# The order of the last four output tiles in a fused attention and feed-forward kernel

## Chip, cores and metric

One NeuronCore of a Trainium2 chip runs the whole kernel. The metric is the device time of one execution in microseconds; the time before is the median of three runs.

## What is computed

The input x has 2048 rows of 448 columns. It is normalised per row, and the output is x plus two branches that both read the normalised rows: attention with 16 heads of 28 columns in a causal window of 256 rows, and a gated feed-forward layer of 1792 hidden columns.

```
xn = layernorm(x)
q, k, v = split(xn @ wqkv)                      # 16 heads of 28
A = softmax(q k^T * 28**-0.5, causal, window 256) v @ wo
B = (gelu(xn @ w_gate) * (xn @ w_up)) @ w_down
out = x + A + B
```

All inputs and the output are bfloat16.

## The kernel before

The rows are worked on in four blocks of 512 (`qb` 0 to 3), each of four row tiles of 128, so row tiles 0 to 15. For each block the kernel makes the attention of that block, which ends in `oN` (four groups of 128 partitions by 512 rows, on SBUF), and the hidden layer `hT` (14 groups of 128 by 512). The output of a row tile is then 18 matmuls that add into one PSUM tile `po`: 14 with `hT` and the weights `wd`, four with `oN` and the weights `wo`, each 448 columns wide. `gen_down` issues them, as a generator that yields after every step, so that for blocks 0 to 2 these matmuls are woven into the attention of the block that follows. The order of everything is written out by hand; there is no scheduler.

For the last block (`qb` 3) nothing follows. Its `gen_down` runs alone at the end, after a check value (`flag`) has been made on VectorE. The terms come in three groups: `main` (ten groups of `hT` that are made early), `late` (the four of `hT` that come from the last two gates, made at line 501) and `os` (the four of `oN`, whose last rows arrive by small transfers that SyncE issues at lines 351 and 356, through a buffer in device memory). `part` issues some terms of one tile (line 393), `whole` all of them, and `end` is called behind the last one: VectorE adds the rows of x to `po` into `res` (line 382), `give` hands the PSUM bank back, and SyncE issues the transfer of `res` to the output (line 384). There are two `res` buffers; the second half of the last tile has a buffer of its own (tag `wa`).

Before, the last block begins three tiles (12, 13, 14) in three of the four single PSUM banks: main of 12 and 13, late of 12 and 13, main and late of 14, then the attention terms of the three, each followed by its add and its transfer. Tiles 13 and 14 are issued as two matmuls of 224 columns for each term (`ws`). Tile 15 follows in two halves of 224 columns, each with its 18 terms, its own PSUM bank, its add and its transfer.

After 48 steps of this generator each engine loads the check value into a register (line 887). Behind the generator GpSimd copies from the last result, VectorE writes one value (lines 890 to 892), and every engine branches on the check value at line 897: where it is 1, as here, a long general path is jumped over. Each engine then waits for its queues and meets the others in a closing barrier (line 1018).

A second PSUM pool (`phase[0].pool`, tag `s`) holds two buffers of two banks each; the last tiles that use them are the gates `gt` of the feed-forward layer, read by ScalarE at line 496.

Of the kernel before, what the change touches and what calls it, by code (L numbers as in the profile page):

```python
# [12 lines left out]
bf16 = mybir.dt.bfloat16  # L13
f32 = mybir.dt.float32
i32 = mybir.dt.int32

S, D, H, Dh, F = 2048, 448, 16, 28, 1792
P = 128
NT = S // P
NF = F // P  # L20
QB, NB = 512, 4
# [6 lines left out]
def kernel(  # L28
# [11 lines left out]
    nc = tc.nc  # L40
# [4 lines left out]
    work = fast.enter_context(tc.tile_pool(name="work", bufs=3))  # L45
# [3 lines left out]
    phase = [None]  # L49
# [152 lines left out]
    held = {}  # L202

    def take(name, cols=QB, tag=None):

        tag = tag or spare[0]
        spare.remove(tag)  # L210
        ps = psum.tile([P, QB], f32, name=name, tag=tag, bufs=1)[:, 0:cols]
        held[id(ps)] = tag, ps
        return ps

    def give(*tiles):
        for ps in tiles:
            spare.append(held.pop(id(ps))[0])
# [94 lines left out]
    def gen_pairs(qb, order):  # L312

        def v_pair(t):
            two = [take("pv", D) for _ in range(2)]
            for c in range(7):
                for hi, ps in enumerate(two):
                    r = slice(64 * hi, 64 * hi + 64)
                    w = wv[r, 3, :] if c == 6 else wv[r, c // 2, :] if c % 2 == hi else wvs[r, c // 2, :]
                    nc.tensor.matmul(ps, lhsT=xchunk(qb, hi, c, (t + hi) * P, P), rhs=w, start=c == 0, stop=c == 6,  # L320
                                     tile_position=(64 * hi, 0), skip_group_check=True)
                if c < 6:
                    yield
            for i in range(2):
                v_copy(t + i, two[i], nc.vector.tensor_copy if i or not t % 4 or qb == 1 else nc.scalar.copy)
            yield

        def qk_pair(g):
            two = [take("p" + part) for part in "qk"]
            for c in range(7):  # L330
                for hi, ps in enumerate(two):
                    r, hs = slice(64 * hi, 64 * hi + 64), slice(4 * g, 4 * g + 4)
                    w = w3p[r, hs, :] if c == 6 else (wqp, wkp)[hi][r, c // 2, hs, :] if c % 2 == hi else wsq[r, c // 2, hs, :]
                    nc.tensor.matmul(ps, lhsT=w.rearrange("p h d -> p (h d)"), rhs=xchunk(qb, hi, c, qb * QB, QB), start=c == 0,  # L334
                                     stop=c == 6, tile_position=(64 * hi, 0), skip_group_check=True)
                if c < 6:
                    yield
            qk_copies(qb, g, *two, nc.vector.tensor_copy if (g != 1) == (qb == 1) else nc.scalar.copy)
            yield

        return chain(*(v_pair(4 * qb + n) if kind == "v" else qk_pair(n) for kind, n in order))
# [25 lines left out]
    def gen_down(qb):  # L367

        hT, oN = hTs[qb], oNs[qb]
        fs = [(hT, wd, f) for f in range(NF)]  # L370
        main, late, os = fs[0:5] + fs[7:12], [fs[f] for f in (5, 12, 6, 13)], [(oN, wo, g) for g in range(4)]

        def begin(tt, lo=0, up=D):
            return tt, take("po", up - lo), lo, up

        def end(tt, po, lo, up):
            t, w = 4 * qb + tt, up - lo
            if lo:
                res = work.tile([P, 2 * QB], bf16, name="res", tag="wa", bufs=1)
            else:  # L380
                res = work.tile([P, D], bf16, name="res", bufs=2)
            nc.vector.tensor_tensor(out=res[:, 0:w], in0=po[:, 0:w], in1=x_sb[:, t, lo:up], op=ALU.add)  # L382
            give(po)
            nc.sync.dma_start(out=outv[:, t, lo:up], in_=res[:, 0:w])
            last_res[:] = [res]

        def part(o, terms, start=False, stop=False):
            tt, po, lo, up = o
            w = up - lo
            ws = (0, w // 2, w) if 4 * qb + tt in (NT - 3, NT - 2) else (0, w)  # L390
            for n, (x, wt, k) in enumerate(terms):
                for a, b in zip(ws, ws[1:]):
                    nc.tensor.matmul(po[:, a:b], lhsT=x[:, k, tt * P:(tt + 1) * P], rhs=wt[:, k, lo + a:lo + b],  # L393
                                     start=start and n == a == 0, stop=stop and n == len(terms) - 1, skip_group_check=True)
                if stop and n == len(terms) - 1:
                    end(*o)
                yield

        def whole(terms, *o):
            yield from part(begin(*o), terms, True, True)  # L400

        if qb < NB - 1:
            two = [begin(tt) for tt in range(2)]
            for o in two:
                yield from part(o, main + late, True)
            for o in two:
                yield from part(o, os[0:3])
            for tt, po, *_ in two:
                r = slice(64 * tt, 64 * tt + 64)
                nc.tensor.matmul(po, lhsT=oN[r, 3, tt * P:(tt + 1) * P], rhs=wo[r, 3, :], start=False, stop=True,  # L410
                                 tile_position=(64 * tt, 0), skip_group_check=True)
            for o in two:
                end(*o)
            yield
            for tt in (2, 3):
                yield from whole(main + late + os, tt)
        else:
            three = [begin(tt) for tt in range(3)]
            for terms, start in ((main, True), (late, False)):
                for o in three[0:2]:  # L420
                    yield from part(o, terms, start)
            yield from part(three[2], main + late, True)
            for o in three:
                yield from part(o, os, False, True)
            for lo, up in ((0, D // 2), (D // 2, D)):
                yield from whole(main + late + os, 3, lo, up)

    def new_hT(qb):
        hT = blk.tile([P, NF, QB], bf16, name="hT", tag="hT")
# [369 lines left out]
    for qb in range(NB):  # L799
# [4 lines left out]
        if qb == 0:  # L804
# [3 lines left out]
            w = gen_pairs(1, (("v", 0), ("v", 2), ("k", 0), ("k", 1), ("k", 2)))  # L808
# [4 lines left out]
                    [lambda: stat(11), (w, 7), lambda: rstd(8, 4), "sums", "inverse", (w, 7)]]  # L813
        else:
            d = gen_down(qb - 1)
            if qb < 3:
                u = gen_pairs(qb + 1, (("v", 0), ("k", 0), ("v", 2), ("k", 1), ("k", 2)))
# [64 lines left out]
    nc.vector.tensor_reduce(out=ok1, in_=okr, axis=AX.X, op=ALU.min)  # L882
    nc.vector.tensor_copy(out=flag[:, :], in_=ok1)
    last = gen_down(NB - 1)
    for _ in range(48):
        next(last)
# [136 lines left out]
```

## Time and profile before

| | |
|---|---|
| median of three runs | 214.37 us (214.35 to 214.7) |
| span of the profiled execution | 213.1 us |
| the median less that span | 1.27 us |
| PE busy | 207.6 us, 97% |
| VectorE, ScalarE, GpSimd busy | 157.5, 131.6, 48.6 us |
| output transfers | 15 of 112 KB, 2 of 56 KB |

The profile gives the span from the first to the last instruction, not a device time for that execution; the device time of the runs is 1.27 us longer than the span. PE is TensorE, PEld its weight loads, DVE VectorE, ACT ScalarE, POOL GpSimd, SP SyncE; a q behind the name is the engine's sequencer, which reads the instructions and waits for semaphores ahead of the engine. A row of a timeline gives the start and the length in us, the engine, the line of the kernel, what is written and read, and the count; in brackets stand the idle time before it and who ended it. Queue q1 is that of the transfers, q8 and q14 are loads of instructions.

### The profile page before, as it was taken

The numbers are of one execution on the slowest core, as the hardware profiler recorded it, in microseconds if no ns is written. First come the engines' busy times: TensorE is split into PE (matmuls) and PEld (weight loads), VectorE is DVE, ScalarE is ACT, GpSimd is POOL, SyncE is SP. The second block draws the span as 40 slices with busy tenths as digits, with TensorE's granted clock in tenths as the row PEclk, the third lists the DMA queues.
The fourth block names the chain that finished last, engine by engine and source line by source line (L and its number), as shares of the span: only waits on it lengthen the run. The fifth ranks groups of instructions, "written<-read, shape, count | busy, mean of one in ns | idle before, by whom it ended". The sixth has DMA issues, their size and how long they took to land.

```text
span 213.1 us, 6428 instructions
## 1 busy us (share of the span) xinstructions
PE 207.6 (97%) x2722; PEld 101.2 (47%) x2722; DVE 157.5 (74%) x355; ACT 131.6 (62%) x123; POOL 48.6 (23%) x86
## 2 busy tenths in 40 slices
PE   7999999999999999999999999999999999999992
PEld 2433444444454545444445445444445444544992
DVE  7899998999767985796536997495483898479531
ACT  4699578566777977423777887532676877665000
POOL 5287658451000220041000201022000022006001
PEclk9999999999999999999999999999999999999998
DMA  6999969979420101003421000001000101000011
GB/s 184 280 221 215 106 172 220 243 241 171 110 53 25 37 20 26 8 5 65 74 74 46 25 0 29 20 0 30 16 3 0 47 4 45 6 0 0 26 45 49
DMA packets 23993, 15.67 MB, mean 74 GB/s; under 512 B 9208, under 2 KB 23832, under 8 KB 23960
## 3 DMA queue, kind: packets, MB, share of 16 engines
q1 hardware_dynamic: 22918, 14.87, 31.2%
q8 instruction: 22, 0.36, 0.7%
q10 hardware_dynamic: 1042, 0.34, 0.7%
q14 instruction: 11, 0.09, 0.1%
HBM read 9.26 MB, written 2.41 MB: 55 GB/s over the span
## 4 chain that ended last, share of the span: by engine, by line
PE 94%; DVE 1%; ACT 1%; DMA 1%; issue 1%; DVEq 0%; ACTq 0%
PE po L393 26%; PE gt L456 20%; PE u L456 12%; PE ue L456 8%; PE pq L334 7%; PE sc L652 6%; PE ov L624 5%; PE pv L320 4%; PE pq L191 2%; PE pv L191 1%; DMA x_sb<-in_A_x_dram 1%; ACT p_sb L656 1%; DVE st L155 1%; PE s L191 1%; PE pk L191 1%
## 5 line engine op out<-in xcount | busy, mean ns | idle before, releaser
L656 ACT ACTIVATE p_sb<-sc 128x2048 bf16<-128x2048 f32 x39 | 73.2, 1878 | 20.5 <-PE sc L652 13.5
L496 ACT ACTIVATE p_sb<-gt 128x1024 bf16<-128x1024 f32 x28 | 28.7, 1025 | 33.6 <-PE gt L456 30.7
L591 POOL TENSOR_TENSOR oN<-oc,l 128x512 bf16<-128x512 f32 x16 | 21.5, 1355 | 120.0 <-DVE l L604 120.0
L393 PE MATMUL po<-wd,hT 128*128 128x448 bf16 (+1 forms) x266 | 46.2, 324 | 0.0
L456 PE MATMUL gt<-xnT,wg 64*128 64x512 bf16 x224 | 45.6, 376 | 0.0
L456 PE MATMUL gt<-xsw,wg 64*128 64x512 bf16 x168 | 40.7, 376 | 0.0
L504 DVE TENSOR_TENSOR hT<-p_sb,u 128x512 bf16<-128x512 bf16 x34 | 21.9, 677 | 16.0 <-PE u L456 15.8
L572 DVE TENSOR_TENSOR p_sb<-p_sb,masks 128x256 bf16<-128x256 bf16 (+1 forms) x90 | 27.8, 363 | 7.6 <-ACT p_sb L656 7.6
L393 PEld LDWEIGHTS <-hT 128*128 128x128 bf16 x266 | 24.5, 98 | 16.8 <-issue 2.2
L456 PEld LDWEIGHTS <-wg 64*128 64x128 bf16 x392 | 19.0, 94 | 22.5 <-issue 0.2
L456 PEld LDWEIGHTS <-wu 64*128 64x128 bf16 x392 | 18.7, 94 | 22.4 <-issue 0.8
L456 PE MATMUL u<-xnT,wu 64*128 64x512 bf16 x136 | 28.1, 376 | 0.0
L456 PE MATMUL u<-xsw,wu 64*128 64x512 bf16 x102 | 24.7, 376 | 0.0
L382 DVE TENSOR_TENSOR res<-po,x_sb 128x448 bf16<-128x448 f32 (+1 forms) x17 | 9.8, 592 | 11.6 <-PE po L393 9.3
L456 PE MATMUL ue<-xnT,wu 64*128 64x512 bf16 x88 | 18.0, 377 | 0.0
L652 PE MATMUL sc<-qT,kT 28*64 28x320 bf16 (+7 forms) x648 | 16.4, 261 | 0.1
L456 PE MATMUL ue<-xsw,wu 64*128 64x512 bf16 x66 | 16.4, 377 | 0.0
L582 POOL TENSOR_SCALAR_AFFINE_SELECT p_sb<-p_sb 128x512 bf16<-128x512 bf16 (+1 forms) x21 | 14.2, 702 | 6.6 <-ACT p_sb L656 6.5
L609 DVE TENSOR_TENSOR oc<-oc,ov 128x512 f32<-128x512 f32 x12 | 8.2, 681 | 8.7 <-ACT oc L608 8.7
L652 PEld LDWEIGHTS <-kT 28*64 28x64 bf16 (+1 forms) x648 | 7.5, 102 | 13.3 <-issue 12.0
L393 PE MATMUL po<-wo,oN 128*128 128x448 bf16 (+1 forms) x70 | 13.0, 320 | 0.0
L473 DVE CAST hT<-ue 128x512 bf16<-128x512 f32 x18 | 11.6, 679 | 1.9 <-PE ue L456 1.8
(108 smaller groups left out, 276.9 us busy)
## 6 DMA issues: line engine op xcount, KB each, us to landing
out_dram<-res SPq DMA_DIRECT2D x15, 112.0 KB
x_sb<-in_A_x_dram SPq DMA_DIRECT2D x3, 448.0 KB
wd<-in_B_w_down_dram SPq DMA_DIRECT2D x3, 448.0 KB
xsw<-xnT SPq DMA_DIRECT2D x6, 192.0 KB
wu<-in_B_w_up_dram SPq DMA_DIRECT2D x2, 560.0 KB
wg<-in_B_w_gate_dram SPq DMA_DIRECT2D x2, 448.0 KB
wg<-in_B_w_gate_dram SPq DMA_DIRECT2D x2, 336.0 KB
wraw<-in_A_wqkv_dram SPq DMA_DIRECT2D x2, 252.0 KB
```

What stands on the lines that cost most here:

```text
L334: nc.tensor.matmul(ps, lhsT=w.rearrange("p h d -> p (h d)"), rhs=xchunk(qb, hi, c, qb * QB, QB), start=c == 0, stop=c == 6, tile_position= ...
L393: nc.tensor.matmul(po[:, a:b], lhsT=x[:, k, tt * P:(tt + 1) * P], rhs=wt[:, k, lo + a:lo + b], start=start and n == a == 0, stop=stop and ...
L456: nc.tensor.matmul(ps, lhsT=w[64 * hi:64 * hi + 64, c, p * P:(p + 1) * P], rhs=xchunk(qb, hi, c, qb * QB, QB), start=c == 0, stop=c == 6, ...
L473: copy(out=hTs[qb][:, p + 7 * i, :], in_=us[i])
L496: nc.scalar.activation(out=ges[p][:, :, :], in_=gt[:, :, :], func=ACT.Gelu_apprx_tanh)
L504: nc.vector.tensor_tensor(out=hT[:, p + 7 * i, :], in0=ge[:, i, :], in1=u, op=ALU.mult)
L572: nc.vector.tensor_tensor(out=reg, in0=reg, in1=m, op=ALU.mult)
L582: nc.gpsimd.affine_select(out=reg, in_=reg, pattern=mid + [[1 if diag else -1, min(w, P)]], compare_op=ALU.is_ge, fill=0.0, base=0 if diag ...
L591: nc.gpsimd.tensor_tensor(out=oN[:, g, :], in0=oc[:, :], in1=inv, op=ALU.mult)
L624: nc.tensor.matmul(ov[half or 0][32 * j:32 * j + 32, q0:q0 + nq], lhsT=v_sb[r, kt, 4 * g + j, :], rhs=p_sb[r, j, col:col + nq], start=n == ...
L652: nc.tensor.matmul(ss[k0:k0 + nk, j, col:col + nq], lhsT=kT[r, g, kt * P + k0:kt * P + k0 + nk], rhs=qT[r, g, ring(qb).start + q0:ring(qb) ...
L656: nc.scalar.activation(out=p_sb[:, :, 0:ncol], in_=ss[:, :, 0:ncol], func=ACT.Exp, scale=SCALE)
```

## The change

Only the last block and `end` are touched. Whole tiles are one matmul per term again (`ws` goes, 36 matmuls fewer). Two tiles are begun, not three: main and late of 12 and 13. Tile 15 gets two PSUM tiles in the two-bank pool, `first` and `last`, one for each half. Main and late of `first` come next, then the attention terms of 12, 13 and `first`, each with its add and transfer; then main of `last`; then the whole of tile 14; then the last eight matmuls, late and attention of `last`. There are four `res` buffers. `give` is called only for PSUM tiles that came from `take`.

```diff
             if lo:
                 res = work.tile([P, 2 * QB], bf16, name="res", tag="wa", bufs=1)
             else:
-                res = work.tile([P, D], bf16, name="res", bufs=2)
+                res = work.tile([P, D], bf16, name="res", bufs=4)
             nc.vector.tensor_tensor(out=res[:, 0:w], in0=po[:, 0:w], in1=x_sb[:, t, lo:up], op=ALU.add)
-            give(po)
+            if id(po) in held:
+                give(po)
...
         def part(o, terms, start=False, stop=False):
             tt, po, lo, up = o
             w = up - lo
-            ws = (0, w // 2, w) if 4 * qb + tt in (NT - 3, NT - 2) else (0, w)
             for n, (x, wt, k) in enumerate(terms):
-                for a, b in zip(ws, ws[1:]):
-                    nc.tensor.matmul(po[:, a:b], lhsT=x[:, k, tt * P:(tt + 1) * P], rhs=wt[:, k, lo + a:lo + b],
-                                     start=start and n == a == 0, stop=stop and n == len(terms) - 1, skip_group_check=True)
+                nc.tensor.matmul(po[:, 0:w], lhsT=x[:, k, tt * P:(tt + 1) * P], rhs=wt[:, k, lo:up],
+                                 start=start and n == 0, stop=stop and n == len(terms) - 1, skip_group_check=True)
...
-            three = [begin(tt) for tt in range(3)]
+            two = [begin(tt) for tt in range(2)]
             for terms, start in ((main, True), (late, False)):
-                for o in three[0:2]:
+                for o in two:
                     yield from part(o, terms, start)
-            yield from part(three[2], main + late, True)
-            for o in three:
+            first, last = ((3, phase[0].pool.tile([P, 2, QB], f32, name="pl", tag="s")[:, 0, 0:D // 2], lo, lo + D // 2)
+                           for lo in (0, D // 2))
+            yield from part(first, main + late, True)
+            for o in (*two, first):
                 yield from part(o, os, False, True)
-            for lo, up in ((0, D // 2), (D // 2, D)):
-                yield from whole(main + late + os, 3, lo, up)
+            yield from part(last, main, True)
+            yield from whole(main + late + os, 2)
+            yield from part(last, late + os, False, True)
```

## The prediction

> **What bounds the kernel now.** I read the page first, then the chain of waits of the last 18 us (the change touches nothing earlier), then one by one the engines that meet there.
>
> ```profile
> span 213.1 us, 6428 instructions
> PE 207.6 (97%) x2722; PEld 101.2 (47%) x2722; DVE 157.5 (74%) x355; ACT 131.6 (62%) x123; POOL 48.6 (23%) x86
> ...
> 195.31 13.88 PE po L393 x126
> 209.19 0.02 issue
> 209.21 0.39 DVE res L382
> 209.60 0.99 issue
> 210.59 0.08 DVEq L897
> ```
>
> PE is busy 97% of the span, and the last block is no exception: the 126 matmuls of the output tiles stand on the chain back to back from 195.31 to 209.19 us, with no other engine between them. Behind them come one add of 0.39 us and then 3.5 us in which nothing computes (209.60 to 213.1). So there are two places to gain: the pace of those matmuls, and what stands between the last add and the end. I call the row tiles by their number, 12 to 15; E is the end of the last matmul, 209.19.
>
> The second place first. The rows are SP's issues of the last three outputs, in the order of time (start, length), and the group of all 17 output issues (min/median/max ns):
>
> ```profile
> 207.39 0.33 SPq L384 DMA_DIRECT2D out_dram<-res  x1
> 208.44 0.33 SPq L384 DMA_DIRECT2D out_dram<-res  x1
> 209.63 0.85 SPq L384 DMA_DIRECT2D out_dram<-res  x1
> L384 SPq DMA_DIRECT2D out_dram<-res x17: 332/361/847, 62.4 to 209.6; - x17
> ```
>
> Sixteen issues take 0.33 to 0.38 us and only the very last, a half tile like the one before it, takes 0.85. That is 0.52 us in which SP stands still. What else ran then:
>
> ```profile
> q8 instruction: 1, 0.02, 103.0%
> ...
> q8 instruction: 1, 0.02, 5.7%
> ...
> DMA  0000000154889998643100000000000000000000
> ...
> DMA packets 12, 0.01 MB, mean 11 GB/s; under 512 B 4, under 2 KB 12, under 8 KB 12
> ...
> DMA  1000015263878987979696674642201000000000
> ```
>
> These are five rows of DMA queries. The first covers 208.4 to 208.5: there a load of code (queue q8) begins. The second covers 208.4 to 210.2: it takes 5.7% of 16 engines for 1.8 us, which is 1.64 us of one DMA engine, to 210.1. The third is the DMA share in 40 bins of 209.1 to 210.0: the first half of tile 15, issued at 208.44, moves its packets from bin 7 to bin 20, so 0.82 us after its issue, done 1.1 us after it. The fourth covers 210.0 to 210.8: only 12 packets, 8 of them above 512 B, so rows of tile 14, which was issued at 207.39 and should long have been out. One engine, held by the code load, kept its share of tile 14. The last covers 210.9 to 211.4: the last half moves at 210.97 to 211.28, 1.34 us after its issue. I read this so: SP could not place its third output in a row on an engine that still held two, and the issue ended, at 210.48, 0.38 us after the code load did.
>
> Who loads code there, and who waits for the landing:
>
> ```profile
> L897 PEldq COMPARE_BRANCH  x1: 392/392/392, 207.3 to 207.3; - x1
> L897 SPq COMPARE_BRANCH  x1: 57/57/57, 210.5 to 210.5; - x1
> L897 SPq EVENT_SEMAPHORE  x8: 17/17/17, 211.1 to 211.7; - x8
> L1018 SPq EVENT_SEMAPHORE  x10: 17/28/28, 211.8 to 213.0; - x10
> ```
>
> PE's sequencer reads the branch behind the last matmul at 207.3, far ahead of PE, and the code load begins 1.15 us later. SP, after its last issue, branches at 210.5, walks through eight waits on the output queues (211.1 to 211.7; the last is the last output's) and then through the closing barrier to 213.0. That walk starts when the last issue ends, so the 0.52 us stand fully on the path.
>
> **The change part by part.** The profiled execution spans 213.1 us; the median of the runs is 214.37, so 1.27 us lie around the span, and I take changes of the span one to one to the median.
>
> Matmul pace. The rows are a whole tile in the middle of the kernel (18 matmuls of 448 columns) and tile 15 in halves:
>
> ```profile
> 64.01 2.82 PE L393 MATMUL po<-wd,hT 128*128 128x448 bf16 x14
> 66.67 0.92 PE L393 MATMUL po<-wo,oN 128*128 128x448 bf16 x4
> ...
> 205.56 1.50 PE L393 MATMUL po<-wd,hT 128*128 128x224 bf16 x14
> 206.90 0.55 PE L393 MATMUL po<-wo,oN 128*128 128x224 bf16 x4
> 207.28 1.50 PE L393 MATMUL po<-wd,hT 128*128 128x224 bf16 x14
> 208.63 0.55 PE L393 MATMUL po<-wo,oN 128*128 128x224 bf16 x4
> ```
>
> From start to start, 14 whole matmuls take 66.67 - 64.01 = 2.66, 0.190 us each; 14 halves take 1.34, 0.0957 each, 0.1914 a pair. The change makes 36 pairs of tiles 13 and 14 whole: 36 x 0.0014 = 0.05 us less, between nothing and 0.1 by the rounding of the starts. The Trainium skill, "TensorE: Matmul & The Clock Gate", section "Wait — 56ns, not 53.3ns?", puts a fixed 2.5 ns on every warm matmul beyond its columns; by it the gain would be an estimated 36 x 2.5 ns = 0.09 us, inside my bounds. Reordering itself costs PE nothing if nothing is late. So I check what each moved step needs:
>
> ```profile
> 194.62 2.93 DVE L501 TENSOR_TENSOR hT<-p_sb,hT 128x1024 bf16<-128x1024 bf16 x3
> 195.40 1.02 ACT L496 ACTIVATE p_sb<-gt 128x1024 bf16<-128x1024 f32 x1 [0.49 <-PE gt L456]
> 195.24 8.19 PE L393 MATMUL po<-wd,hT 128*128 128x448 bf16 x70
> 203.27 2.45 PE L393 MATMUL po<-wo,oN 128*128 128x448 bf16 x20
> 197.90 1.35 SPq L356 DMA_DIRECT2D oN<-o  x4
> 204.88 5.60 SPq L384 DMA_DIRECT2D out_dram<-res  x5
> 206.73 0.62 DVE L382 TENSOR_TENSOR res<-po,x_sb 128x448 bf16<-128x448 f32 x1 [1.11 <-DMA out_dram<-res]
> ```
>
> The late terms still begin after 20 x 0.190, at 199.0, and their hT is done at 197.55. The two new PSUM tiles take the buffers of the last gates, which ACT has read by 196.42; they are needed at 200.6. The attention terms move: before they start at 203.27, now after 28 whole and 14 half matmuls, 195.24 + 5.32 + 1.34 = 201.9. They need the four transfers into oN, issued by 199.25. A landing takes at most 1.85 us, from the first output (issued 204.88) to the add that waited for its buffer (206.73). So oN is there by 201.1, 0.8 us early. What hides it is the 14 half matmuls of tile 15 and the earlier ones; were oN later than 201.9, the excess would stand on PE in full.
>
> Four result buffers. They serve all blocks, but only two adds of the whole trace waited for a buffer: the add of tile 14 waited 1.11 us for the first output to land, and the next one 0.66 us. Both waits go, but PE waited for neither, so that alone is worth nothing; what is late next for these adds is the matmul before them.
>
> The order on the queues. DVE now adds 12, 13, the first half of 15, 14, the last half; SP issues in that order, the first half past tile 14. Eight halves, 0.77 us, lie between the end of tile 14 and E, which is now 209.14. So tile 14 ends at 208.37, its add of 0.62 at 209.03, its issue of 0.33 at 209.36; the last add runs 209.16 to 209.55 and the last issue starts at 209.58. Both queues are free in time, by 0.1 and 0.2 us.
>
> The code load. PE's sequencer runs ahead by a number of matmuls:
>
> ```profile
> L393 PEldq EVENT_SEMAPHORE  x2: 51/51/51, 201.6 to 201.7; - x2
> ```
>
> These two waits stand in the code right before the first attention term (203.27), and the branch (207.3) behind the last matmul, which starts at 208.63 + 0.29 = 208.92. Both are 1.6 us, or 17 halves, ahead. After the change 17 matmuls back from the last start are seven halves and ten whole ones: 0.67 + 1.90 = 2.57 us. The branch is read at 206.3, the code load runs from 207.45 to 208.4 or 209.1, and in that stretch no output is in flight: the first half of 15 was issued before 205.6 and tile 14 starts moving at 209.03 + 0.82 = 209.85. So SP's last issue takes 0.33 again: 0.52 us less. What is late next is the landing: the last half's packets end 1.1 us after its issue, at 210.7, behind those of tile 14, which are out by 210.4 on the same engines. A landing of at most 1.85 us gives 211.4; by the packets, some 0.5 after them, 211.2. SP reaches its eighth wait 1.2 us after its branch, at 211.15. Of the 0.52 us I count 0.50, with 0.3 and 0.55 as ends.
>
> Weighed against a rule: the Trainium skill, "Perfetto Trace Analysis", section "DMA Instruction — HWDGE (DVE, Sync)", says that the length shown for such an issue holds the wait for the descriptor generator and the writing of descriptors into a buffer that can be full. By it 0.85 us is a wait and not work, as in my reading; had it been the generator that another queue held, the time would not move. No row shows another queue issuing at 209.6.
>
> Sum: 0.05 + 0.50 = 0.55 us, 214.37 to 213.8.
>
> **The rivals.** A, the forecast: the stall of the last issue goes, 213.8, between 213.7 (0.1 + 0.55 off) and 214.05 (0 + 0.3 off).
>
> B, the issue stays long. The 0.85 us appear once in the trace, and a reason beside the code load (the jump to far code right behind it, say) would stay. For it: no row names SP's releaser there. Against it: the end of the wait fits the end of the code load, and 16 other issues are short. Then only the pace remains: 214.32, between 214.27 and 214.37.
>
> C, slower: the code load moves into the last two outputs and not ahead of them. From its start at 208.45 to SP's eighth wait (211.7) it is 3.25 us; if it still catches the last outputs, the end shifts with its start. It is 1.15 us behind the branch, so it decides at the sequencer's lead: a branch read after 207.75, 1.4 us ahead of E, is slower by over 0.43; with a lead of six matmuls the branch is at 208.4, the load at 209.55, and the kernel at 215.4. For it: the sequencer must now wait for oN some 20 matmuls in advance, and the lead shrinks there. Against it: 44 matmuls follow, 18 of them whole, which give it time to fill up again.
>
> **How the numbers follow.** A has 0.62, B 0.23, C 0.15. What a measurement can tell from no change is about 0.2%, 0.43 us, so A counts as faster where it ends below 213.94: 0.58 of its 0.62. Faster 0.58, same 0.27 (B and the weak end of A), slower 0.15 (C). The range holds A and B, 0.85 in all, with 0.1 of noise on either side: 213.6 to 214.45.
>
> **What would show it.** Right: the last output issue at about 0.33 us; PE's branch near 206.3 and the q8 load near 207.5; 90 matmuls in the last block instead of 126, without an idle row on PE near 201.9; SP's eight waits ending near 211.1. B is right if the last issue is still 0.85 with no code load beside it. C is right if the q8 load begins after 208.9. The forecast is wrong altogether if PE waits for oN, or if the span loses less than the last issue does.

## The result, and the profile after

The new kernel takes 214.22 us in the median of 22 runs (214.04 to 214.75), beside 214.68 us for the kernel before (22 runs, 214.19 to 215.97). The ratio is 0.9975, with a 95% interval from 0.9965 to 0.9985. On the 214.37 us of the three first runs that is 213.83, for a forecast of 213.8; in microseconds it is 0.54 less, between 0.32 and 0.75. The runs of the kernel before also spread wider, over 1.78 us against 0.71.

The page of the profile after, and its chain of waits from 195 us to the end:

```profile
span 212.6 us, 6354 instructions
PE 207.7 (98%) x2686; PEld 97.8 (46%) x2686; DVE 157.4 (74%) x355; ACT 131.6 (62%) x123; POOL 48.8 (23%) x86
...
195.47 5.40 PE po L392 x28
200.87 1.34 PE pl L392 x14
202.21 1.51 PE po L392 x8
203.72 1.34 PE pl L392 x14
205.06 3.40 PE po L392 x18
208.47 0.78 PE pl L392 x8
209.25 0.02 issue
209.27 0.39 DVE res L382
209.67 0.99 issue
210.66 0.08 DVEq L899
```

The new order stands there piece by piece: 12 and 13 whole, the first half of 15 in `pl`, and so on to the last eight halves, 90 matmuls with nothing between them. They take 13.78 us on the chain (195.47 to 209.25); the 126 before took 13.88. From the start of the first to the start of the last it is 13.58 us against 13.67, so 0.09 less. The block begins 0.15 us later than before (195.39 against 195.24), and that difference is there from the first 8 us on, before anything that the change touches. So the end of the last matmul, E, is even 0.06 us later (209.24, where the timeline before has 209.18), and what is won is won behind it.

SP's issues of the last two outputs, the group of all 17, PE's code load (a DMA query of 207.6 to 207.7), then the branches and the walk of the waits:

```profile
209.16 0.33 SPq L385 DMA_DIRECT2D out_dram<-res  x1
209.69 0.33 SPq L385 DMA_DIRECT2D out_dram<-res  x1
L385 SPq DMA_DIRECT2D out_dram<-res x17: 332/362/421, 62.5 to 209.7; - x17
...
q8 instruction: 1, 0.02, 60.2%
...
L899 SPq EVENT_SEMAPHORE  x8: 17/17/17, 210.6 to 211.2; - x8
L899 PEldq COMPARE_BRANCH  x1: 486/486/486, 206.4 to 206.4; - x1
L899 SPq COMPARE_BRANCH  x1: 58/58/58, 210.1 to 210.1; - x1
L1020 SPq EVENT_SEMAPHORE  x10: 17/28/28, 211.3 to 212.6; - x10
```

No issue is long any more: the last takes 0.33 us, not 0.85. PE's branch is read at 206.4 and its code load runs from 207.68 for 0.96 us (a packet is counted whole where it begins, so 60.2% of 16 engines for 0.1 us is 0.96 us of one engine), over 0.5 us before the next output is issued. From E to the end of the span it was 3.91 us and is 3.39: the 0.52 us of the last issue.

### The profile page after: what moved, and what is told of

It reads as the page before. It is cut to its first block, busy times and chain, and to the rows that moved or that the text cites. A ratio compares the mean times of both kernels' runs of the same rounds, so it can differ in the third digit from the quotient of the medians.

```text
span 212.6 us, 6354 instructions
## 1 busy us (share of the span) xinstructions
PE 207.7 (98%) x2686; PEld 97.8 (46%) x2686; DVE 157.4 (74%) x355; ACT 131.6 (62%) x123; POOL 48.8 (23%) x86
## 4 chain that ended last, share of the span: by engine, by line
PE 97%; ACT 1%; issue 1%; DVE 0%; DVEq 0%; ACTq 0%
PE po L392 24%; PE gt L458 20%; PE u L458 12%; PE ue L458 8%; PE pq L334 7%; PE sc L654 6%; PE ov L626 5%; PE pv L320 4%; PE wps L150 2%; PE pq L191 2%; PE pl L392 2%; PE pv L191 1%; ACT p_sb L658 1%; PE s L191 1%; PE pk L191 1%
## 5 line engine op out<-in xcount | busy, mean ns | idle before, releaser
L392 PE MATMUL po<-wd,hT 128*128 128x448 bf16 x210 | 43.3, 353 | 0.0
L392 PEld LDWEIGHTS <-hT 128*128 128x128 bf16 x238 | 21.9, 98 | 19.4 <-issue 2.2
L382 DVE TENSOR_TENSOR res<-po,x_sb 128x448 bf16<-128x448 f32 x15 | 9.0, 619 | 11.5 <-PE po L392 11.0
L392 PE MATMUL po<-wo,oN 128*128 128x448 bf16 x54 | 12.0, 352 | 0.0
```

Source lines behind the costliest of these rows:

```text
L392: nc.tensor.matmul(po[:, 0:w], lhsT=x[:, k, tt * P:(tt + 1) * P], rhs=wt[:, k, lo:up], start=start and n == 0, stop=stop and n == len(term ...
```

## The experiments

Theory L is that of the prediction: PE's branch starts a load of code on one DMA engine, and while it holds that engine SP's last issue stands still; the new order moves the load out of the way. The rivals are named with each run. All ratios are to the kernel before.

**The kernel before once more.** Is the long issue a chance event?

> The kernel before, unchanged, for a second profile. Theory L: the code load again begins about 0.7 us ahead of the end of the last matmul, and the last issue again takes 0.75 to 0.9 us. If the long issue was a chance event of one execution, it takes 0.33 us here.

The last issue, and the code load (query of 208.6 to 208.7):

```profile
209.81 0.50 SPq L384 DMA_DIRECT2D out_dram<-res  x1
...
q8 instruction: 1, 0.02, 80.8%
```

It is there again, but with 0.50 us; the load, at the same place 0.7 us ahead of E, took 1.29 us and not 1.65. It misses the expected 0.75 to 0.9. So the stall is regular in place and not in size. It need not be the cause of the wide spread of the runs before: the two stalls differ by 0.35 us and the runs by 1.78, and the two kernels without this code load, further down, still spread over 1.21 and 0.97 us.

**Four buffers alone, in the old order.**

```diff
-                res = work.tile([P, D], bf16, name="res", bufs=2)
+                res = work.tile([P, D], bf16, name="res", bufs=4)
```

> The order before, with four result buffers and nothing else. Theory L (PE's code load catches the outputs, and SP cannot place a third output in a row on an engine that still holds two): the add of tile 14 no longer waits 1.11 us for a buffer, its output is issued near 206.6 and out by 208.0, before the code load at 208.45. The load then holds only the first half of tile 15, so the last issue takes 0.33 us and not 0.85, and the span loses 0.2 to 0.5 us (ratio 0.9976 to 0.999). Rival O (the gain came from the new order, the buffers are worth nothing, as the prediction had it): last issue 0.85, ratio 1.000.

```profile
209.56 0.81 SPq L384 DMA_DIRECT2D out_dram<-res  x1
...
q8 instruction: 1, 0.02, 99.6%
```

The ratio is 0.9999 (0.9986 to 1.0012). Tile 14 was issued at 206.54 and had landed by 208.35, so the load (208.39, 1.59 us) held the first half of tile 15 alone, and the last issue still took 0.81 us, where theory L had expected 0.33. The buffers are worth nothing, as the prediction had it, but the picture of a *third* output that finds no room falls: one held output was enough.

**Whole matmuls alone, in the old order.**

```diff
-            ws = (0, w // 2, w) if 4 * qb + tt in (NT - 3, NT - 2) else (0, w)
+            ws = (0, w)
```

> The order before, tiles 13 and 14 as whole matmuls, nothing else. Theory L: tile 15 still ends the block in halves, so the branch is still read 1.6 us ahead of the last matmul, the code load still comes 0.7 us ahead of its end and the last issue stays at 0.85 us; only the pace is gained, 0.05 to 0.09 us (ratio 0.9996). Rival W (fewer instructions are what moves the load out of the way): the load moves, the last issue takes 0.33, 0.6 us less (ratio 0.997).

The last piece of PE on the chain, the last issue and the load:

```profile
195.34 13.79 PE po L393 x90
...
209.57 0.74 SPq L384 DMA_DIRECT2D out_dram<-res  x1
...
q8 instruction: 1, 0.02, 95.9%
```

13.79 us against 13.88 for the 126 matmuls: the pace is worth 0.09 us. The branch is read at 207.2, 1.87 us ahead of E as before, the load comes at 208.39 and the issue is long. The ratio, 1.000 (0.9989 to 1.0011), cannot tell 0.09 us from nothing. Fewer instructions alone do not move the load; rival W falls.

**The new order, with 13 and 14 in halves again** (the two loops over `ws` put back into `part`).

> The new order with tiles 13 and 14 in halves again, so 126 matmuls. Pace: 0.05 to 0.09 us slower than the new kernel. The branch is read 17 halves ahead again, about 1.7 us before the end of the last matmul, so the code load begins about 0.6 us before it. Theory L: the load then comes before tile 14 moves (its issue is at the end of the last matmul, its packets 0.8 us later) and holds at most that one output, so the last issue takes 0.33 us: 0.4 to 0.5 us less than before (ratio 0.998). Rival P (the load must lie well ahead of the last outputs, which needs the whole matmuls): the last output is held again, ratio 1.000.

```profile
209.65 0.40 SPq L385 DMA_DIRECT2D out_dram<-res  x1
...
q8 instruction: 1, 0.02, 74.2%
```

The ratio is 0.9985 (0.9977 to 0.9994). With 17 halves of lead the load begins 0.71 us ahead of E again and lasts 1.19 us, to 0.48 behind it; the last issue, at 0.45 behind E, is caught by its end and takes 0.40, where 0.33 was expected. Rival P falls: the order alone brings most of the gain (3.45 us from E to the end of the span, against 3.91 before and 3.39 in the new kernel), with the load where it was before; it is shorter here, and only tile 14 is near it. The whole matmuls add 0.09 us of pace and move the load clear of the last issue.

**The load moved, and nothing else.** Loads of the check value into a PE register ahead of the branch delay only PE's sequencer:

```diff
     for _ in last:
         pass
+    for _ in range(3):      # or 1, 2
+        nc.values_load(flag[0:1, 0:1], engines=[mybir.EngineType.PE], min_val=0, max_val=1)
```

> The new kernel with one more load of the check value into a PE register ahead of PE's branch, as a control for the run with three. The branch comes 0.5 to 0.8 us later, the code load then runs from about 1.0 to 0.0 us before the end of the last matmul, still ahead of the last issue at 0.46 us after it. Theory L: last issue 0.33 to 0.45 us, ratio 0.9975 to 0.998. If the added instruction itself cost time, the ratio would be nearer to 1.

> The new kernel with two more loads of the check value into a PE register ahead of PE's branch, between the runs with one (branch 2.07 us ahead of the end of the last matmul, code load 0.71 us ahead of it, last issue 0.33) and with three (branch 0.59 ahead, load 1.31 behind it, the last two outputs landing 3.45 and 3.64 us behind it). The branch should come 1.33 us ahead and the load at or up to 0.3 us behind the end of the last matmul. Theory L: with a load of 0.95 to 1.3 us the last issue ends about 0.38 us after it, so it takes 0.9 to 1.5 us and the span is 0.6 to 1.2 us longer than with one (ratio 1.001 to 1.004). Rival O: last issue 0.33, ratio 0.998.

> The new kernel with three more loads of the check value into a PE register right ahead of PE's branch: no engine but PE's sequencer has more to do. Each takes its sequencer about 0.5 us or a little more, so the branch is read 1.5 to 2.4 us later and the code load begins near the end of the last matmul (0.1 us before to 0.8 us after it). Theory L (an output issue beside the code load cannot end before about 0.38 us after the load): with a load of 1.0 to 1.6 us the last issue takes 0.9 to 2 us and the whole gain is lost again, 0.3 to 1.3 us slower than the new kernel (ratio to the kernel before 0.999 to 1.004). Rival O (the order and the distance of the outputs decide): last issue 0.33 us, ratio 0.9975.

For one, two and three such loads in turn: PE's branch, the code load (queries of 208.2, 208.9 and 210.6 to 0.1 us later), the last issue and SP's eight waits. E is at 208.95, 209.03 and 209.33.

```profile
L901 PEldq COMPARE_BRANCH  x1: 500/500/500, 206.9 to 206.9; - x1
q8 instruction: 1, 0.02, 59.1%
209.40 0.33 SPq L385 DMA_DIRECT2D out_dram<-res  x1
L901 SPq EVENT_SEMAPHORE  x8: 17/17/17, 210.3 to 211.0; - x8
...
L901 PEldq COMPARE_BRANCH  x1: 498/498/498, 207.7 to 207.7; - x1
q8 instruction: 1, 0.02, 77.6%
209.49 1.04 SPq L385 DMA_DIRECT2D out_dram<-res  x1
L901 SPq EVENT_SEMAPHORE  x8: 17/17/17, 211.1 to 211.8; - x8
...
L901 PEldq COMPARE_BRANCH  x1: 407/407/407, 208.7 to 208.7; - x1
q8 instruction: 1, 0.02, 59.2%
209.79 0.33 SPq L385 DMA_DIRECT2D out_dram<-res  x1
L901 SPq EVENT_SEMAPHORE  x8: 17/17/17, 210.7 to 213.0; - x8
```

These are the runs that decide. The matmuls, the order and the distances of the outputs are the same in all three (the last block takes 13.58 us from its first to its last start in each). With one load the branch comes 2.07 us ahead of E. The code load then begins 0.71 us ahead of E, where it began in the old order, but it takes 0.95 us and ends at 0.24 behind E, 0.22 us before the last issue; nothing changes behind E: 3.39 us to the end, ratio 0.9983 (0.9973 to 0.9993). Tile 14, with no output queued ahead of it, was issued in 0.33 us beside this load (from 0.08 ahead of E to 0.26 behind it). With two the code load lies across the last issue, which takes 1.04 us; 4.10 us to the end, ratio 1.0005 (0.9989 to 1.0020; 1.001 to 1.004 was expected), the whole gain is gone. With three it begins 1.31 us behind E, after the last issue, which is short again; but now both outputs wait for their share on the held engine, and SP stands in its walk until 213.0: 5.03 us to the end, ratio 1.005 (1.0033 to 1.0066). For three I had expected the load earlier, a long issue and at most 1.004; the issue was as short as rival O said, but the time was not its 0.9975. The branch came 2.2 us later than without them, as expected, but the load 1.9 us behind it instead of 1.15 to 1.25. Rival O, that the order and the distances alone decide, falls. They do count: with the load at its old place, 0.71 us ahead of E, the old order has a long issue and the new one, in the run with one load, has none.

**No branch, no far code** (the fallback for out-of-range sums, and with it the branch, is left out), in both orders:

```diff
-    with tc.If(n_ok < 1, preferred_fallthrough_block=True, label="general"):
-        general_path(tc, ...)
```

> The kernel before without the branch and the general path behind it (the fallback for out-of-range sums is left out; order and outputs of the last tiles as before). Theory L: no far code, so no code load by PE after 208, the three last outputs are issued at the same distances and the last takes 0.33 us: 0.5 us less there, and another 0.5 us as SP's jump of 0.48 us goes (ratio 0.995). Rival T (three outputs within 2.3 us are by themselves too many for the queue, with or without a code load): the last issue still takes 0.85 us, 0.5 us less in all (ratio 0.9977).

> The new kernel without the branch and the general path (the fallback is left out), beside the kernel before without them (ratio 0.9973, last issue 0.33 us, 2.91 us from the end of the last matmul to the end of the span). Theory L: without a code load nothing is left of the change but the pace of the matmuls, so the same 2.9 us behind the last matmul, and a block 0.09 us shorter: ratio 0.997. Rival O (the order itself is worth 0.4 us or more): the end behind the last matmul is shorter by that much, ratio 0.995.

The last issue in the old and in the new order, then the stretch 52 to 56 us of the kernel before and of the old order without the branch (stretch and length, then the busy us and the count of PE, PEld, DVE, ACT and POOL, the granted clock, the DMA share and GB/s):

```profile
210.21 0.33 SPq L384 DMA_DIRECT2D out_dram<-res  x1
210.42 0.33 SPq L385 DMA_DIRECT2D out_dram<-res  x1
...
52.00:56.00 4.00, 4.00 (x59) 1.84 (x56) 3.33 (x11) 3.15 (x3) 0.31 (x1) 1.00 0.38 72
52.00:56.00 4.00, 3.67 (x37) 1.62 (x32) 3.61 (x9) 3.92 (x3) 0.31 (x1) 1.00 0.41 68
```

Without the branch there is no q8 load behind 208, and the three outputs at their old distances are issued in 0.33 us each: rival T falls. E to the end is 2.91 us in both orders, so nothing of the change is left but the pace of the matmuls: 0.9973 (0.9958 to 0.9989) in the old order, 0.9969 (0.9954 to 0.9985) in the new one. For the old order I had expected 0.995: the 1.0 us behind E did go, but the last block begins 0.58 us later than before, and 0.33 us of that is lost near 52 us, where PE is busy 3.67 us of 4.00 in place of all four. (The new order without the branch loses 0.40 us between 52 and 60.)

The traces show what happened there, and it is the same stall on another engine. The rows are ACT's last two issues of `o` in the kernel before and in the old order without the branch, then for the latter the code load (query of 49.3 to 49.4), PE's wait, and SP's second output issue of the kernel with the code load beside it (query of 62.7 to 62.8):

```profile
48.81 0.76 ACTq L351 DMA_DIRECT2D o<-oN  x2
...
48.92 1.80 ACTq L351 DMA_DIRECT2D o<-oN  x2
q8 instruction: 1, 0.02, 60.9%
52.81 0.42 PE L652 MATMUL sc<-qT,kT 28*64 28x320 bf16 x16 [0.33 <-ACT p_sb L496]
63.51 0.83 SPq L384 DMA_DIRECT2D out_dram<-res  x1
q8 instruction: 1, 0.02, 77.1%
```

A code load runs from 49.34 for 0.98 us; the second of ACT's issues, begun at 49.28, takes 1.43 us and ends 0.40 us after it. So ACT starts its next work at 50.82, and not at 49.67 as before (0.11 us of this lies ahead of the issues), and PE waits 0.33 us for it. The new order without the branch has the same: an issue of 1.35 us that ends 0.40 us after the load, and PE waits 0.24 us. Why the loads and the issues meet there without the branch was not followed. The output issue at 63.51 ends 0.38 us after the load beside it; in four more runs (four buffers, one and three register loads, the new order without the branch) the second output issue took 0.54 to 0.77 us and ended 0.37 to 0.39 us after a load. So the stall needs neither PE's last branch nor the end of the kernel. Not every long issue is of this kind: with two buffers in the new order the same issue of ACT took 0.87 us and ended before the load beside it.

**Two buffers in the new order.**

> The new order with two result buffers as before. The add of the first half of tile 15 waits for the first output to land, about 1.3 us, and its output is issued some 3.2 us ahead of the end of the last matmul, not 3.84; PE waits for neither. Theory L and the prediction: the code load lies where it did, 1.56 us ahead, nothing is in its way when the last two outputs are issued, ratio 0.9975 as with four. If the buffers were needed in the new order, the ratio would be nearer to 1.

The ratio is 0.9981 (0.9970 to 0.9993), the last issue 0.33 us, the load 1.56 us ahead of E as with four. VectorE's add of the first half of tile 15 waited 1.2 us for a buffer and its output was issued 3.28 us ahead of E and not 3.84; PE waited for neither.

The runs in which the load ran into the last issue, in us behind E:

| kernel | load begins | load lasts | load ends | last issue | issue ends | from load to issue end |
|---|---|---|---|---|---|---|
| before | -0.72 | 1.65 | 0.93 | 0.85 | 1.30 | 0.37 |
| before, again | -0.71 | 1.29 | 0.58 | 0.50 | 0.96 | 0.38 |
| four buffers, old order | -0.71 | 1.59 | 0.88 | 0.81 | 1.27 | 0.39 |
| whole matmuls, old order | -0.72 | 1.54 | 0.82 | 0.74 | 1.19 | 0.37 |
| halves, new order | -0.71 | 1.19 | 0.48 | 0.40 | 0.85 | 0.37 |
| new, two more loads | -0.12 | 1.24 | 1.12 | 1.04 | 1.50 | 0.38 |

Less the 0.33 us of an undisturbed issue, that is as if SP went on some 0.05 us after the code load ended. It also says when a load is felt: an undisturbed last issue ends 0.79 us behind E, so a load must end later than about 0.41. In the new kernel, with two buffers, and with one register load it ends at -0.60, -0.61 and 0.24, and the issue is short.

## Why the prediction was right

- **What bounds.** Right. PE has no gap in the last block, and the two places named, the pace and the last issue, are where the time came from: 0.09 and 0.52 us, together 0.61 in the profile, of which 0.15 us of a later start hides some in the span (0.46). By the letter this meets one of my signs of being wrong, that the span loses less than the last issue does: 0.46 against 0.52. The sign left no room for a start that differs between two executions; that difference is there by 8 us, and of the time behind E the full 0.52 us went.
- **The pace.** Forecast 0.05 us within 0 to 0.1, measured 0.09 (13.79 against 13.88 us). The rows that I used were rounded to 10 ns, too coarse for a difference of 1.4 to 2.5 ns a pair. The estimate of 0.09 us from the 2.5 ns per matmul of the Trainium skill ("TensorE: Matmul & The Clock Gate", "Wait — 56ns, not 53.3ns?") was the better value; the trace agrees with it.
- **The last issue and its cause.** Right in place: 0.50 forecast of 0.52, 0.52 measured. The size is partly luck: in the four profiles of the old order with the branch the last issue took 0.85, 0.50, 0.81 and 0.74 us, so 0.17 to 0.52 us too long, and I had read the longest. That the code load is the cause is shown: the stall goes with the branch, and comes back when the load alone is moved onto the issue. Moving the load ahead is not all that helps: at its old place it took 0.95 and 1.19 us in the new order, where no output was queued as it began, and 1.29 to 1.65 in the old, where one or two were. Whether the queued outputs lengthen it was not tested. The detail was wrong: it need not be a third output behind two held ones, since one held output stalls the issue as well. What exactly is full stays open; in the kernel before, the first half of tile 15 was issued in 0.33 us beside the beginning of the load, although tile 14 had a share on that engine.
- **The sequencer's lead.** Right: the branch at 206.4 for 206.3, the load at 207.7 for 207.45, ending at 208.64 within 208.4 to 209.1.
- **What covers the moved steps.** Right: the attention terms begin at 202.05 and PE does not wait for `oN`; both queues were free when the last add and the last issue came.
- **Four buffers at nothing.** Right in both orders, within what the runs can tell (0.9999 for four alone; 0.9981 for two in the new order beside 0.9975).
- **Rival B** fell with the profile after, whose last issue is short with the same jump behind it. **Rival C** did not happen, but the runs with two and three loads are that case. Its price was too high, since it took the load at 1.64 us and the eighth wait 3.25 us behind its start: with three loads the load took 0.95 and SP was through 2.3 us behind its start; with two the branch came 1.38 us ahead of E, and it cost 0.19 us behind E, not the 0.43. (In the argument against C, 48 matmuls follow from the first attention term on, 26 of them whole, not 44 and 18.)
- **The sum.** 0.55 us forecast; 0.54 (0.32 to 0.75) measured. The interval leaves out zero but not the 0.43 us that I had named as the bound.

## What to carry to other kernels

Look at the lengths of DMA issues, not only at who waits: one issue of 0.85 us, where the sixteen others took 0.33 to 0.38, held 0.52 of the 0.61 us, and its partner stood on another queue, that of the instruction loads. In the twelve traces ten output issues took over 0.45 us, five of them at the end of the kernel, and all ten ended 0.37 to 0.39 us after a code load. PE's sequencer read its branch 1.87 us before the last matmul ended, and the load that followed took a DMA engine for 0.95 to 1.65 us. The number of matmuls still queued sets when the branch is read (about 17 in both orders), so the order and the size of the last matmuls can move the load away from the last outputs.

## What the hardware showed that I had not expected

- PE's code load of 16 KB took 0.95 to 0.96 us in the four runs with the branch in which it made no output issue long, and 1.19 to 1.65 us in the six in which it did, so the stall beside it varies in size. Which of the two lengthens the other is not shown.
- The load seems to hold its engine before its own first record. In the new kernel tile 14, issued 0.08 us ahead of E, had moved all its 128 rows by 1.2 us behind E. In the run with three loads, issued at the same distance, eight of the rows moved only at 2.25 to 2.87, though the load's record begins at 1.31 and ends at 2.26; SP saw them land at 3.46. Only the records' times speak for this; no run tested it.
